# A masked attention and two feed-forward layers on one core: five token blocks in place of six

## The chip, the cores and the metric

The kernel runs on one core of a Trainium2 chip. The metric is the time of one execution in microseconds of the device; the time before is the median of three runs.

## What is computed

```python
scores = scale * np.matmul(q, k.transpose(0, 1, 3, 2))      # q, k, v: 4 x 8 x 576 x 64
kth = np.partition(scores, -32, axis=-1)[..., -32:-31]      # the 32nd largest of each row
scores = np.where(scores >= kth, scores, -1e9)
attn = np.exp(scores - np.max(scores, axis=-1, keepdims=True))
attn = attn / (np.sum(attn, axis=-1, keepdims=True) + 1e-09)
x = np.matmul(attn, v)                                      # -> 2304 tokens x 512
h = np.maximum(x @ w_in, 0.0);  x = (h * h) @ w_out         # layer 0, 512 -> 2048 -> 512
h = x @ w_in2;  out = np.maximum(0.01 * h, h) @ w_out2      # layer 1, other weights
```

## The kernel before, in words

The attention works on 144 tiles of 128 query rows (one head pair's rows of one unit, cut into 128s), two tiles to a **pair**, so 72 pairs, 0 to 71. `UNITS` lists runs of tokens (batch, first token, count) in the order in which they are worked off; a unit of 256 tokens has 8 pairs, one of 320 tokens 10, one of 64 tokens 2. For each pair TensorE multiplies q and k (L279), VectorE finds the 32 largest of each row with four rounds of MAX8 and MATCH_REPLACE8 (L829, L831), ScalarE and GpSimd (POOL in the profile) mask, exponentiate and scale (L298, L299, L303, L312), TensorE transposes (L317, L330) and, when a head pair of a unit is complete, multiplies with V (L412, L401). The result goes to `x_out` (L433 to L436), which splits each value into a high and a low part, xh and xl. For batches 2 and 3 the scores are made early and kept in DRAM.

The two layers run on **blocks** of tokens (`BLOCKS`). A block is ready once its last token has come out of the attention; tokens of a unit that belong to the next block are kept in `spill` and copied by `unspill` (L118, L452, both on POOL). Each layer of a block takes 16 steps f over the 2048 hidden features. A step has 12 matmuls h (L580: four chunks of the 512 inputs, three products of high and low parts) as wide as the block has tokens, then ScalarE and POOL (VectorE in the last block, by `LEAK2` and `GLD`) apply the nonlinearity and split it into gh and gl. In layer 0 it has 12 matmuls acc of the block's width (L618); in layer 1, where gh and gl are the stationary operand, 3 of 512 columns for each 128 tokens (L620). The matmuls acc of a step come one step late (`LAG`).

Block 0 meets the weights for the first time: for its 32 steps they are loaded raw, put together from two 32-bit halves (ScalarE L513, L514, VectorE L518, L519), split (ScalarE L523, POOL L526) and stored to DRAM. Later blocks load 1 MB of split weights for each step.

What sets the order: events have slots, 16 to a pair. At each slot the attention's events are written out, and then as much of the ready block as its `rate` allows, which is its number of matmul groups divided by the number of slots until the next block is ready. When a block becomes ready, what is left of the one before is written out first. The attention's events are put some places forward, and a scheduler then sets the order of each engine, which works its list in that order. `PIPE` says how many blocks run both layers one after the other; the ones behind it are interleaved: in the kernel before, layer 0 of block 4 runs alone, then come layer 0 of block 5, layer 1 of block 4 and layer 1 of block 5. `SETS` says which tiles hold a block's xh and xl: set 0 serves blocks 0, 2 and 4, set 1 blocks 1 and 3, and block 5 has tiles of its own (set 2).

Of the kernel before, what the change touches and what calls it, by code (L numbers as in the profile page):

```python
# [24 lines left out]


UNITS = [
    (0, 0, 256), (0, 256, 256), (0, 512, 64), (1, 0, 256), (1, 256, 320),
    (2, 0, 256), (3, 0, 256), (2, 256, 320), (3, 256, 320),
]  # L30

BLOCKS = [512, 256, 384, 512, 256, 384]

SETS = (0, 1, 0, 1, 0, 2)

PIPE = 4

SPILL = 128


NATIVE = 3
# [22 lines left out]
KLO_D = ((0, 0), (0, 1))  # L64
QLO_D = (0,)

LEAK2 = 5
GLD = 5


@with_exitstack
def topk_attention_moe_moe2_kernel(
# [98 lines left out]
    for i in range(NE):  # L171
        ebufs.append(const.tile([P, S], F, tag=f"e{i}", name=f"e{i}"))
    spill = const.tile([P, NHP, SPILL], F, tag="spill", name="spill")
    early_ctx = ExitStack()
# [195 lines left out]
    g = 0  # L370
    for n in BLOCKS:
        blocks.append(dict(g0=g, n=n, idx=len(blocks)))
# [4 lines left out]
    def block_x(blk):  # L377

        if "x" not in blk:
            i = SETS[blk["idx"]]  # L380
            m = max(x["n"] for x in blocks if SETS[x["idx"]] == i)
            if i == 2:
# [73 lines left out]
    for j in range(len(blocks)):  # L456
        if j < PIPE:
            groups.append([(j, 0), (j, 1)])
        elif j == PIPE:
            groups.append([(j, 0)])  # L460
        else:
            groups.append([(j, 0), (j - 1, 1)])
    if PIPE < len(blocks):
        groups[-1].append((len(blocks) - 1, 1))
# [93 lines left out]
    def moe(j, layer):  # L558
# [6 lines left out]
        for f in range(NF + LAG):  # L565
            conv = iter(())
            if f < NF:
# [21 lines left out]
                if layer == 0:  # L589
                    ACT.activation(a[:, 0:n], h[:, 0:n], AF.Relu)  # L590
                    ACT.activation(a[:, 0:n], a[:, 0:n], AF.Square)
                elif j >= LEAK2:
                    ACT.activation(a[:, 0:n], h[:, 0:n], AF.Copy, scale=0.01)
                    DVE.tensor_tensor(a[:, 0:n], a[:, 0:n], h[:, 0:n], op=OP.max)
                else:
# [4 lines left out]
                ACT.activation(gh[:, 0:n], a[:, 0:n], AF.Copy)  # L600
                (DVE if j >= GLD else POOL).tensor_tensor(gl[:, 0:n], a[:, 0:n], gh.bitcast(F)[:, 0:n],  # L601
                                                          op=OP.subtract)
# [302 lines left out]
```

## Time and profile before

| what | us |
|---|---|
| median of three runs | 1217.16 (1215.74 to 1218.06) |
| the profiled execution | 1214.43 |
| its span, first to last instruction | 1212.6 |
| TensorE busy / VectorE busy | 1135.6 / 946.5 |
| ScalarE busy / POOL busy | 908.9 / 728.1 |

The span is read by stages: attention alone until block 0 is ready, block 0 with the conversion of the weights, blocks beside the attention, and blocks alone after the last pair. Busy time of TensorE is that of pipelined matmuls, so that durations of neighbours overlap; what a matmul costs in a stream is the distance from one start to the next.

### The profile page before, as it was taken

Reading aid. Unit: us, or ns where it says so; the run is one execution under the profiler, and the core shown is the slowest. Engines: PE = TensorE matmul, PEld = TensorE weight load, DVE = VectorE, ACT = ScalarE, POOL = GpSimd, SP = SyncE. Lnnn points to the kernel's source line nnn. Section 1 sums busy time; section 2 is a strip of 40 time slices with the busy share of each in tenths; the row PEclk is TensorE's granted clock in tenths of the full one; section 3 lists DMA queues with packets and bytes.
Section 4 is the critical chain, followed back from the end, with each engine's and each line's share of the span. In section 5 each row is a group of like instructions: output and inputs, shape, how many; then the busy total and the mean of one; then the engine's idle time right before and its main releaser. Section 6 shows DMA issues by size and latency. Waiting matters only on the chain.

```text
span 1212.6 us, 20357 instructions
## 1 busy us (share of the span) xinstructions
PE 1135.6 (94%) x6388; PEld 992.6 (82%) x6388; DVE 946.5 (78%) x1944; ACT 908.9 (75%) x2019; POOL 728.1 (60%) x868
## 2 busy tenths in 40 slices
PE   4788878999789989999999998999999999999998
PEld 3666765887578879989999996888788899998997
DVE  7999999778888899999999999999999920110122
ACT  6889899989999988887877777777777764334322
POOL 7998977667689985477656684545576642004300
PEclk9999997999989999999999999999999999999999
DMA  9665566878889988889988787667576589879974
GB/s 305 232 224 196 197 197 255 279 273 303 307 281 301 315 281 270 291 283 397 343 297 293 279 274 258 213 221 236 182 233 230 192 270 368 259 247 343 350 253 137
DMA packets 110522, 323.24 MB, mean 267 GB/s; under 512 B 17488, under 2 KB 25680, under 8 KB 110416
## 3 DMA queue, kind: packets, MB, share of 16 engines
q1 hardware_dynamic: 107776, 317.24, 77.1%
q10 hardware_dynamic: 2640, 4.72, 1.1%
q8 instruction: 51, 0.84, 0.3%
q14 instruction: 55, 0.45, 0.1%
HBM read 254.54 MB, written 67.37 MB: 265 GB/s over the span
## 4 chain that ended last, share of the span: by engine, by line
PE 54%; ACT 17%; DVE 12%; DMA 4%; POOL 3%; issue 3%; ACTq 0%; SPq 0%; POOLq 0%; DVEq 0%
PE h L580 22%; PE acc L618 11%; PE acc L620 11%; DVE m L829 5%; DVE w L831 4%; PE att L412 3%; PE att L317 3%; ACT e L303 2%; ACT att L514 2%; ACT e L298 1%; ACT wc L513 1%; PE att L401 1%; ACT s L280 1%; ACT stage L280 1%; DVE PTs L323 1%
## 5 line engine op out<-in xcount | busy, mean ns | idle before, releaser
L580 PE MATMUL h<-xh,wi 128*128 128x512 f32 (+2 forms) x1280 | 349.8, 345 | 10.5 <-ACT gb L598 4.4
L829 DVE MAX8 m<-w 128x8 f32<-128x576 f32 x432 | 313.2, 747 | 1.6
L580 PEld LDWEIGHTS h<-xh,wi 128*128 128x128 f32 x1280 | 227.5, 191 | 39.3 <-ACT gb L598 6.2
L601 POOL TENSOR_TENSOR gl<-ga,gh 128x512 fp32r<-128x512 f32 (+2 forms) x160 | 163.0, 1018 | 118.8 <-ACT gh L600 54.0
L299 POOL TENSOR_TENSOR e<-s,e 128x576 f32<-128x576 f32 x144 | 203.2, 1432 | 26.7 <-ACT e L298 24.2
L831 DVE MATCH_REPLACE8 w<-m,w 128x576 f32<-128x576 f32 x288 | 213.1, 742 | 0.8
L580 PE MATMUL h<-xl,wi 128*128 128x512 f32 (+2 forms) x640 | 206.8, 341 | 2.8 <-DVE xl L632 2.6
L618 PE MATMUL acc<-gh,wo 128*128 128x512 f32 (+2 forms) x768 | 154.8, 341 | 0.4 <-ACT gh L600 0.4
L620 PE MATMUL acc<-wo,gh 128*128 128x512 f32 x576 | 151.1, 397 | 0.7 <-ACT gh L600 0.6
L599 POOL TENSOR_TENSOR ga<-ga,gb 128x512 f32<-128x512 f32 (+2 forms) x80 | 81.3, 1017 | 117.0 <-ACT gb L598 116.6
L618 PEld LDWEIGHTS acc<-gh,wo 128*128 128x128 f32 x768 | 125.0, 189 | 10.6 <-ACT gh L600 1.1
L580 PEld LDWEIGHTS h<-xl,wi 128*128 128x128 f32 x640 | 121.0, 190 | 15.3 <-DVE xl L632 5.1
L600 ACT ACTIVATE gh<-ga 128x512 fp32r<-128x512 f32 (+2 forms) x192 | 100.3, 522 | 35.6 <-POOL ga L599 24.2
L303 ACT ACTIVATE e<-e,kf 128x576 f32<-128x576 f32 x144 | 112.4, 781 | 15.6 <-POOL e L299 14.2
L620 PEld LDWEIGHTS acc<-wo,gh 128*128 128x128 f32 x576 | 104.2, 189 | 19.6 <-ACT gh L600 1.2
L298 ACT ACTIVATE e<-s,kf 128x576 f32<-128x576 f32 x144 | 105.8, 777 | 15.4 <-POOL kf L291 13.5
L829 DVE MAX8 m<-s 128x8 f32<-128x576 f32 x144 | 104.5, 747 | 11.9 <-ACT s L280 10.8
L590 ACT ACTIVATE ga<-h 128x512 f32<-128x512 f32 (+2 forms) x96 | 46.8, 487 | 82.5 <-PE h L580 81.8
L831 DVE MATCH_REPLACE8 w<-m,s 128x576 f32<-128x576 f32 x144 | 106.8, 742 | 0.3
L317 PE MATMUL att<-ident,e 128*128 128x128 f32 x576 | 90.3, 285 | 13.1 <-ACT e L303 9.2
L317 PEld LDWEIGHTS att<-ident,e 128*128 128x128 f32 x576 | 70.6, 145 | 27.4 <-ACT e L303 14.9
L312 ACT ACTIVATE e<-e,rc 128x576 f32<-128x576 f32 x108 | 78.0, 770 | 13.6 <-DVE rc L308 13.5
(93 smaller groups left out, 2150.8 us busy)
## 6 DMA issues: line engine op xcount, KB each, us to landing
wi<-wd SPq DMA_DIRECT2D x160, 512.0 KB, 5.0
wo<-wd SPq DMA_DIRECT2D x160, 512.0 KB, 5.2
wraw<-in_w_dram SPq DMA_DIRECT2D x64, 512.0 KB, 5.7
sd<-stage SPq DMA_DIRECT2D x72, 288.0 KB, 2.8
s<-sd SPq DMA_DIRECT2D x72, 288.0 KB, 5.0
wd<-wi SPq DMA_DIRECT2D x32, 512.0 KB, 5.3
wd<-wo SPq DMA_DIRECT2D x32, 512.0 KB, 5.5
kraw<-in_k_dram SPq DMA_DIRECT2D x16, 576.0 KB, 4.6
```

Source lines behind the costliest of these rows:

```text
L298: ACT.activation(e, x, AF.Relu, bias=pr["kf"][:, i:i + 1], scale=-FAR)
L299: cur["pool"] = POOL.tensor_tensor(e, x, e, op=OP.subtract)
L303: ACT.activation(e, e, AF.Exp, bias=pr["nb"][:, i:i + 1], scale=0.125, accum_out=pr["sum"][:, i:i + 1])
L317: PE.transpose(ps[:, j * P:(j + 1) * P], t["e"][:, j * P:(j + 1) * P], ident)
L580: PE.matmul(h[:, 0:n], lhsT=wi[:, w, c * P:(c + 1) * P], rhs=x[c][y][:, 0:n], start=cnt == 0, stop=cnt == 3 * NK - 1)
L599: POOL.tensor_tensor(a[:, 0:n], a[:, 0:n], b[:, 0:n], op=OP.subtract)
L600: ACT.activation(gh[:, 0:n], a[:, 0:n], AF.Copy)
L601: (DVE if j >= GLD else POOL).tensor_tensor(gl[:, 0:n], a[:, 0:n], gh.bitcast(F)[:, 0:n], op=OP.subtract)
L618: PE.matmul(acc[c][:, 0:n], lhsT=wo[:, w, cs], rhs=g[:, 0:n], start=first, stop=last)
L620: PE.matmul(acc[c], lhsT=g[:, cs], rhs=wo[:, w, :], start=first, stop=last)
L829: cur["dve"] = DVE.max(out=m8[:, x, 8 * r:8 * r + 8], in_=t["s"] if r == 0 else t["w"])
L831: cur["dve"] = DVE.match_replace(out=t["w"], in_to_replace=m8[:, x, 8 * r:8 * r + 8], in_values=t["s"] if r == 0 else t["w"], imm_value=NEG)
```

## The change

The six blocks of 512, 256, 384, 512, 256 and 384 tokens become five of 512, 384, 512, 512 and 384. Batch 1 is divided into units of 320 and 256 tokens instead of 256 and 320, so that unit 3 ends with token 896, where block 1 now ends. `PIPE` is 5, so that every block runs its two layers one after the other and none is interleaved. Set 2 is gone: block 4 uses the tiles of blocks 0 and 2. At most 64 tokens spill. `LEAK2` and `GLD` go from 5 to 4, so that they mean the last block as before.

```diff
 UNITS = [
-    (0, 0, 256), (0, 256, 256), (0, 512, 64), (1, 0, 256), (1, 256, 320),
+    (0, 0, 256), (0, 256, 256), (0, 512, 64), (1, 0, 320), (1, 320, 256),
     (2, 0, 256), (3, 0, 256), (2, 256, 320), (3, 256, 320),
 ]
-BLOCKS = [512, 256, 384, 512, 256, 384]
-SETS = (0, 1, 0, 1, 0, 2)
-PIPE = 4
-SPILL = 128
+BLOCKS = [512, 384, 512, 512, 384]
+SETS = (0, 1, 0, 1, 0)
+PIPE = 5
+SPILL = 64
-LEAK2 = 5
-GLD = 5
+LEAK2 = 4
+GLD = 4
```

The blocks are ready after pairs 15, 25, 35, 51, 61 and 71 before, and after pairs 15, 27, 43, 61 and 71 now.

The first place is TensorE from the matmuls with V of pair 42's tiles to the transposes of pair 44 (e_112 and e_113 are pair 43's tiles, e_110 and e_111 pair 44's). Before:

```order
L317 MATMUL att<-ident,e_112 128x128 x4
L618 MATMUL acc<-gl,wo 128x384
L317 MATMUL att<-ident,e_113 128x128 x4
L618 MATMUL acc<-gl,wo 128x384 x3
...
L412 MATMUL att<-PTs,VT 128x256 x8
L618 MATMUL acc<-gh,wo 128x384 x8
L412 MATMUL att<-PTs,VT 128x256
L618 MATMUL acc<-gl,wo 128x384 x4
L317 MATMUL att<-ident,e_110 128x128 x4
L317 MATMUL att<-ident,e_111 128x128 x4
```

and now:

```order
L620 MATMUL acc<-wo,gl 128x512 x3
L580 MATMUL h<-xh_5790,wi 128x512
L412 MATMUL att<-PTs,VT 128x256
L317 MATMUL att<-ident,e_112 128x128 x4
L317 MATMUL att<-ident,e_113 128x128 x4
L330 MATMUL att<-ident,e_112 64x128
L330 MATMUL att<-ident,e_113 64x128
L412 MATMUL att<-PTs,VT 128x256 x9
L317 MATMUL att<-ident,e_110 128x128 x4
L317 MATMUL att<-ident,e_111 128x128 x4
...
L580 MATMUL h<-xh_5790,wi 128x512 x5
```

Before, block 2 (384 columns) runs between the transposes of the two pairs. Now block 1's last matmuls (L620) and three h of block 2 stand ahead of pair 43, no matmul of a block stands between the pairs, and block 2 (xh_5790) goes on behind pair 44.

The second place is VectorE in pair 29 (m_5683 before, m_5429 now; L518 and L519 convert weights, wc). Before:

```order
L829 MAX m_5683<-s_108 128x8
L323 TENSOR_TENSOR PTs<-att,PTs 128x4x128
L829 MAX m_5494<-w 128x8
L831 MATCH_REPLACE w<-m_5683,s_108 128x576
L829 MAX m_5683<-w 128x8
L831 MATCH_REPLACE w<-m_5683,w 128x576
```

and now:

```order
L829 MAX m_5429<-s_108 128x8
L831 MATCH_REPLACE w<-m_5429,s_108 128x576
L829 MAX m_5429<-w 128x8
L323 TENSOR_TENSOR PTs<-att,PTs 128x4x128
L831 MATCH_REPLACE w<-m_5429,w 128x576
L518 SCALAR_TENSOR_TENSOR wc<-att,wc 128x512
L829 MAX m_5429<-w 128x8
L519 SCALAR_TENSOR_TENSOR wc<-att,wc 128x512
```

The conversion, whose last instruction stood just ahead of pair 28's first MAX8, now goes on through pair 29.

The third place is TensorE where the last block's layer 0 ends, behind all of the attention. Before:

```order
L618 MATMUL acc<-gh,wo 128x384 x8
L618 MATMUL acc<-gl,wo 128x384 x4
L580 MATMUL h<-xh_10045,wi 128x256 x8
L580 MATMUL h<-xl_10046,wi 128x256 x4
L618 MATMUL acc<-gh,wo 128x384 x8
L618 MATMUL acc<-gl,wo 128x384 x4
```

and now:

```order
L618 MATMUL acc<-gh,wo 128x384 x8
L618 MATMUL acc<-gl,wo 128x384 x4
L618 MATMUL acc<-gh,wo 128x384 x8
L618 MATMUL acc<-gl,wo 128x384 x4
L580 MATMUL h<-xh_10238,wi 128x384 x8
L580 MATMUL h<-xl_10239,wi 128x384 x4
```

The first h of layer 1 belonged to another block (256 columns) and stood ahead of the last acc; now it belongs to the same block and stands behind it.

## Rows read from the trace of the kernel before

**Rows 1.** The page, busy us (share of the span) of each engine.

```profile
PE 1135.6 (94%) x6388; PEld 992.6 (82%) x6388; DVE 946.5 (78%) x1944; ACT 908.9 (75%) x2019; POOL 728.1 (60%) x868
```

**Rows 2.** Windows by stage: from:to, length, busy us of each engine, clock, DMA.

```profile
0.00:208.80 208.80, 163.62 (x865) 129.47 (x866) 197.67 (x421) 179.45 (x471) 176.84 (x249) 0.94 0.69 229
208.80:448.80 240.00, 226.91 (x1110) 185.26 (x1109) 196.45 (x369) 224.22 (x463) 190.93 (x187) 0.99 0.85 292
448.80:631.40 182.60, 178.91 (x1262) 171.79 (x1261) 180.55 (x382) 149.79 (x352) 110.94 (x145) 1.00 0.89 314
631.40:754.40 123.00, 117.01 (x668) 107.14 (x667) 121.84 (x258) 95.65 (x200) 82.96 (x99) 0.98 0.84 283
754.40:984.00 229.60, 226.61 (x1130) 187.76 (x1129) 217.11 (x457) 177.10 (x347) 131.12 (x142) 1.00 0.66 212
984.00:1207.00 223.00, 222.54 (x1365) 211.18 (x1363) 32.87 (x61) 81.59 (x187) 35.35 (x48) 1.00 0.82 286
```

**Rows 3.** Windows of VectorE's MAX8 alone (L829): from:to, length, busy (count).

```profile
196.10:435.40 239.30, 59.62 (x81) 0.98 0.83 284
435.40:631.40 196.00, 91.81 (x128) 1.00 0.90 315
631.40:728.90 97.50, 45.59 (x64) 0.98 0.84 284
728.90:971.10 242.20, 114.65 (x160) 0.99 0.67 220
```

**Rows 4.** Chain of work that ended last: start, us; twelve matmuls of 512, 384, 256.

```profile
766.23 2.79 PE acc L618 x12
...
972.72 1.45 PE h L580 x12
...
1028.68 2.10 PE h L580 x12
```

**Rows 5.** Timeline of TensorE, hand-over from block 2 to 3: start, us, instructions, idle before.

```profile
739.78 1.11 PE L412 MATMUL att<-PTs,VT 128*128 128x256 f32 x8
740.73 0.86 PE L620 MATMUL acc<-wo,gl 128*128 128x512 f32 x3
...
742.25 1.15 PE L317 MATMUL att<-ident,e 128*128 128x128 f32 x8
743.15 1.66 PE L620 MATMUL acc<-wo,gh 128*128 128x512 f32 x6
...
754.46 1.78 PE L580 MATMUL h<-xh,wi 128*128 128x512 f32 x5
```

**Rows 6.** Timeline and chain at the start of block 0's layer 1.

```profile
336.18 0.79 PE L580 MATMUL h<-xh,wi 128*128 128x512 f32 x1 [3.58 <-ACT gb L598]
...
336.18 5.49 PE h L580 x12
```

**Rows 7.** Timeline of TensorE between block 3's two layers.

```profile
868.41 1.10 PE L580 MATMUL h<-xl,wi 128*128 128x512 f32 x2 [1.15 <-DVE xl L632]
...
870.69 0.51 PE L580 MATMUL h<-xh,wi 128*128 128x512 f32 x1 [0.38 <-ACT gb L598]
```

**Rows 8.** Conversion: VectorE's longest wait; ScalarE's attention lines, busy, mean ns.

```profile
DVE wc L518 <- ACT att L514: 23.8, 18, 3.8
...
L280 ACT ACTIVATE s<-att 128x288 f32<-128x288 f32 x45 | 18.2, 411 | 0.7 <-PE att L279 0.5
L298 ACT ACTIVATE e<-s,kf 128x576 f32<-128x576 f32 x22 | 17.1, 777 | 0.7 <-PE att L330 0.7
L303 ACT ACTIVATE e<-e,kf 128x576 f32<-128x576 f32 x22 | 17.1, 777 | 0.7 <-POOL e L299 0.7
L312 ACT ACTIVATE e<-e,rc 128x576 f32<-128x576 f32 x20 | 14.4, 773 | 0.7 <-DVE rc L308 0.7
```

**Rows 9.** Timeline of POOL where block 2's spilled tokens are copied.

```profile
439.34 0.65 POOL L118 TENSOR_SCALAR xh<-spill 128x64 fp32r<-128x64 f32 x3
```

**Rows 10.** Waits of TensorE after 984: who waited for whom, us, times, longest.

```profile
PE h L580 <- DMA wi<-wd: 0.4, 1, 0.4
```

## The prediction

> **What bounds the kernel now.** I read the page's busy shares first, then a table of windows by stage, then the steps of one line on VectorE, then the timeline of TensorE at one hand-over. A pair is two tiles of 128 query rows; there are 72, numbered 0 to 71, and VectorE runs 8 MAX8 for each.
>
> TensorE is busy for 94% of the span and VectorE for 78% [rows 1], but the stages have different limits [rows 2]. Until 208.8 there is attention alone. From 208.8 to 448.8 block 0 runs with weights that are still being converted: ScalarE is busy 224.2 of 240.0 us, TensorE 226.9, VectorE 196.5, so ScalarE and TensorE are nearly full and VectorE, which could go faster, waits. From 448.8 to 754.4 VectorE is busy 180.6 of 182.6 and 121.8 of 123.0: it sets the pace, and TensorE idles 3.7 and 6.0 us. From 754.4 on TensorE has no more than 3.5 us of idle time until 1207: whatever work it has left then is what the end waits for.
>
> The count of MAX8 gives the pace of the pairs [rows 3]. In the conversion, pairs 18 to 27 take 239.3 us, 23.9 each (80 MAX8; the 81st of that row lies across its edge); the next 16 take 196.0, 12.2 each; 8 more take 97.5, and the last 20 take 242.2, 12.1 each. So pair 44 begins at 631.4 and pair 52 at 728.9.
>
> At 754.46, 25.6 us after pair 52 began, TensorE goes on with block 3, which became complete with pair 51 [rows 5]. From there to its last matmul at 1206.9 are 452.4 us. These two numbers, the 25.6 and the 452.4, carry the sum.
>
> **Prices.** Twelve matmuls take 2.79 us at 512 columns, 2.10 at 384 and 1.45 at 256 [rows 4]: 0.2325, 0.175 and 0.121 us each. A block runs 16 x 36 matmuls of its own width and 16 x 3 of 512 columns for each 128 of its tokens. That is 178.6 us for 512 tokens, 134.3 for 384, 92.0 for 256. A pair of attention costs TensorE 0.90 us for 8 transposes (742.25 to 743.15), about 0.25 for the two short ones and 1.06 for the matmuls with V (8 take 0.95 us, 739.78 to 740.73; nine to a pair) [rows 5]: 2.2 us.
>
> **The change part by part.**
>
> *One block less.* Before, the six blocks cost 2 x (178.6 + 134.3 + 92.0) = 809.8 us of TensorE; after, 3 x 178.6 + 2 x 134.3 = 804.4: 5.4 us less. The tokens are the same, and what goes is the fixed part of a matmul, since 256 columns cost more than half of 512. The Trainium skill (TensorE: Matmul & The Clock Gate, Back-to-back issue gap) gives columns / 2.4 GHz plus 2.5 ns for each matmul; by it 512 columns would cost 215.8 ns, this part would save 1.5 us instead of 5.4, the 86.6 us below would be 82.1 and the predicted time 1216.2. The trace has 232 ns for 512 columns [rows 4] and does not agree, so the sum goes by the trace.
>
> *Loads.* The 32 steps of the block that goes take 64 loads of weights with them. I cost that at nothing: transfers run beside the matmuls, and in the last 223 us TensorE waits for one only once, 0.4 us [rows 10]. That also bounds what their absence can return on the path.
>
> *The point at which blocks become complete.* This is where the change acts. Blocks were complete after pairs 15, 25, 35, 51, 61 and 71; now after 15, 27, 43, 61 and 71. By pair 43 only blocks 0 and 1 (178.6 + 134.3 = 312.9 us) have been on offer, where before three (404.9) had been since pair 35. The order of TensorE shows the result: between the transposes of pairs 43 and 44 no matmul of a block is left. TensorE must wait for attention there and then has block 2, 3 and 4 ahead: 178.6 + 178.6 + 134.3 = 491.5 us. Before, from 754.46, it had blocks 3, 4 and 5: 404.9. That is 86.6 more. It also has 27 pairs of attention ahead instead of 19: 8 x 2.2 = 17.6. So from the hand-over to the end it needs 452.4 + 86.6 + 17.6 = 556.6 us.
>
> If VectorE is no faster than before, the hand-over comes 25.6 us after 631.4, at 657.0, and the last matmul at 1213.6: 6.7 us later than now. The saved 5.4 us and the idle time gained before 657.0 are both inside this number.
>
> *The conversion stretch.* The rate at which block 0 is laid out is set by the pairs until the next block, 12 instead of 10, so about two more pairs share the conversion: the order of VectorE has its last conversion in pair 29 instead of at the start of pair 28. Each of these two no longer costs 12.2 us afterwards. What it costs in the stretch is not in the trace. If TensorE sets it, 3.3 us (2.2 and the scores); if ScalarE does, its work for a pair: two each of 0.78, 0.78 and 0.77 us and four of 0.41 [rows 8] are 6.3, with some 2 us of smaller ones 8.3, at 93% occupancy 8.9; if VectorE's in-order queue does, the whole 12.2. VectorE's longest wait in the stretch is for ScalarE (23.8 us) [rows 8], so I take 8.9 and with it 2 x 3.3, rounded down to 6 us, since the three engines are then loaded more evenly and disturb each other more. The bounds are 0 and 17.
>
> *The end.* Before, block 5's first layer was followed by block 4's second, which waits for nothing. Now block 4's second layer follows its own first, with no attention left to fill the gap. The nearest row is the boundary between block 3's layers: 1.15 and 0.38 us of idle time [rows 7]. I take 1.5; bounds 0 and 1.5.
>
> *A colder start.* After the idle 3.58 us before 336.18, twelve matmuls took 5.49 us instead of 2.79 [rows 6]: TensorE ran at the lower of its two levels, 1.2 GHz. The wait at pairs 43 and 44 is longer than the one at 745 to 754, of which part of such a loss is in the 452.4 already. I add 1.3; bounds 0 and 2.7.
>
> *The x tiles.* Block 4 now reuses the tiles of block 2 (set 0) where block 5 had its own. POOL's copy of the 64 spilled tokens into them stands behind pair 62's subtraction and must wait for block 2's last h matmul; behind it on POOL are block 2's gl, the kf of pair 63 and its subtraction, for which ScalarE's exponentials wait. When block 2's spill went in at 439.34 there was no idle time before it [rows 9]. I take 0; upper bound 5 us, the rest of block 2's last step after pair 61.
>
> *The sum:* 6.7 - 6 + 1.5 + 1.3 = 3.5 us more. The profiled execution lasts 1214.43 us (span 1212.6) and the median of the three runs is 1217.16, so the difference goes on the median: 1220.7.
>
> **The rivals.**
>
> *The conversion gives back more (faster).* If TensorE sets the stretch, two pairs save up to 17 us. From 9.5 us on the kernel is no slower; at 15 the time is 1217.2 + 6.7 - 15 + 2.8 = 1211.7. For it: VectorE idles 43.5 us there. Against: ScalarE is at 93%. Chance 0.17.
>
> *TensorE's sum alone counts (faster).* TensorE is at 94%, so 5.4 us less work would end 5.4 us earlier, at 1211.8. Against: the order empties TensorE at pair 44, and VectorE, at 99%, cannot bring pair 44 sooner by itself. Chance 0.08.
>
> *Nothing comes back, and POOL waits (slower).* The conversion gives 0 and the copy into set 0 stalls POOL: 6.7 + 2.8 + 3 = 12.5, so 1229.7. Chance 0.20.
>
> *The forecast,* gains of 3 to 9 us in the conversion: 1217.7 to 1223.7. Chance 0.55.
>
> **How the numbers follow.** About 0.2%, 2.4 us, is what a measurement of this kernel can tell from no change. Of the forecast's 0.55, some 0.24 lies inside it and the rest is slower; of the first two rivals 0.22 is faster, 0.03 inside or slower; the third is slower. That makes faster 0.22, same 0.25, slower 0.53. The low end, 1210, takes in both faster rivals; the high end, 1231, the third with the bounds of the boundary and of the clock.
>
> **What would show it.** MAX8 of pair 44 near 625 on VectorE (631 if the conversion gave nothing, below 620 for the first rival); some 10 us of idle TensorE just before block 2's first layer; no idle time on TensorE worth naming from there on; 556 us or a little more from there to the last matmul; a tail after the last matmul with V of about 224 us of block work (now 220). It would be wrong if block 2 began before 645, if TensorE idled again after pair 45, or if POOL sat for more than 3 us before its copy from spill.

## The result, and the profile after

The changed kernel takes 1232.89 us (median; 1230.37 to 1233.45) against 1217.61 beside it: 1.0114 of the time before, 95% interval 1.0093 to 1.0136, 14 to 15 us slower. The prediction was 1220.7 us in a range up to 1231. The direction was right; the time lies above the range. The profiled execution took 1230.37 us, its span is 1228.6 and its last matmul ends at 1222.8 (before: 1206.9), so 15.9 us are to be explained in the profiles, of which the prediction had 3.5.

The page, as [rows 1]:

```profile
PE 1142.4 (93%) x5812; PEld 968.0 (79%) x5812; DVE 948.3 (77%) x1940; ACT 897.7 (73%) x1915; POOL 717.8 (58%) x812
```

TensorE has 576 matmuls and 5.4 us of work less than before, and yet is busy 6.8 us longer: its matmuls ran slower (mean granted clock of the span 0.974, before 0.983). The windows by stage of the kernel after; columns as in [rows 2], the stages cut at its own points: block 0 until 474.0, block 1 until pair 44, the hand-over, blocks beside attention, blocks alone.

```profile
0.00:208.80 208.80, 164.31 (x865) 129.78 (x866) 197.80 (x421) 179.26 (x470) 177.28 (x249) 0.94 0.69 228
208.80:474.00 265.20, 245.95 (x1197) 201.12 (x1197) 227.78 (x435) 247.82 (x512) 201.71 (x195) 0.97 0.79 274
474.00:631.40 157.40, 155.59 (x925) 146.72 (x924) 151.38 (x316) 121.24 (x262) 96.83 (x115) 1.00 0.77 261
631.40:658.80 27.40, 18.48 (x92) 14.88 (x90) 27.02 (x58) 19.17 (x38) 15.07 (x21) 0.75 0.63 213
658.80:984.00 325.20, 320.95 (x1572) 265.94 (x1572) 308.17 (x648) 245.98 (x476) 182.20 (x197) 0.98 0.66 222
984.00:1222.80 238.80, 237.14 (x1170) 209.52 (x1168) 36.13 (x66) 83.11 (x159) 44.67 (x37) 1.00 0.61 207
```

The fourth row is the new wait: in 27.40 us TensorE is busy 18.48, at a granted clock of 0.75, while VectorE is busy 27.02. It is where the prediction put it. Its timeline on TensorE (start, us, instructions, in brackets the idle time before and who ended it):

```profile
643.12 0.39 PE L412 MATMUL att<-PTs,VT 128*128 128x256 f32 x1 [1.13 <-DVE PTs L340]
647.88 1.97 PE L317 MATMUL att<-ident,e 128*128 128x128 f32 x8 [4.38 <-ACT e L312]
...
652.51 2.58 PE L412 MATMUL att<-PTs,VT 128*128 128x256 f32 x9 [2.23 <-DVE PTs L323]
655.80 1.97 PE L317 MATMUL att<-ident,e 128*128 128x128 f32 x8 [0.71 <-ACT e L312]
658.22 0.64 PE L330 MATMUL att<-ident,e 128*64 128x128 f32 x2 [0.45 <-DVE xf L418]
658.76 2.50 PE L580 MATMUL h<-xh,wi 128*128 128x512 f32 x5
```

Block 2 goes on at 658.76, not 651, and its first five matmuls take 2.50 us where those of block 3 took 1.78 [rows 5]. The eight transposes take 1.97 us for both pairs. In the kernel before, those of pair 51 took 1.15 [rows 5], but those of pair 52, just ahead of the block, took 1.97 too:

```profile
752.41 1.97 PE L317 MATMUL att<-ident,e 128*128 128x128 f32 x8 [1.28 <-ACT e L312]
754.17 0.63 PE L330 MATMUL att<-ident,e 128*64 128x128 f32 x2
```

The windows of VectorE's MAX8 (L829), as [rows 3], for pairs 30 to 37 before, then for pairs 30 to 37 and 38 to 43 now (66 MAX8 where two neighbours lie across the edges):

```profile
461.20:560.20 99.00, 45.93 (x66) 1.00 0.87 301
...
452.80:559.70 106.90, 46.19 (x64) 1.00 0.73 247
559.70:631.20 71.50, 33.79 (x48) 1.00 0.83 287
```

Pair 30 begins at 452.8, where before it was 461.2: 8.4 us gained in the conversion. But the next 8 pairs take 106.9 us, 13.4 each instead of 12.4, and pair 44 begins at 631.2, as before. From 475 to 550 TensorE is busy for every microsecond of three windows of 25, and what VectorE waits for most between 450 and 562 is ScalarE's copy of scores (L280):

```profile
DVE m L829 <- ACT s L280: 4.0, 4, 1.4
```

Behind the hand-over TensorE loses time where layers change. Between block 2's two layers it waits for VectorE's xl, and the matmuls behind it come 0.43 us apart instead of 0.23, at a granted clock of 0.50, the lower level; between block 4's two layers it waits for ga, and the clock stays at 1.00 (the windows of both places stand last):

```profile
772.98 0.50 PE L580 MATMUL h<-xl,wi 128*128 128x512 f32 x1 [0.83 <-DVE xl L632]
774.17 0.49 PE L580 MATMUL h<-xl,wi 128*128 128x512 f32 x1 [0.69 <-DVE xl L632]
...
776.43 0.63 PE L580 MATMUL h<-xl,wi 128*128 128x512 f32 x1
776.86 0.63 PE L580 MATMUL h<-xh,wi 128*128 128x512 f32 x1
...
1157.43 0.44 PE L580 MATMUL h<-xh,wi 128*128 128x384 f32 x1 [1.17 <-DVE ga L594]
...
776.00:781.00 5.00, 5.00 (x12) 3.86 (x13) 5.00 (x14) 2.25 (x4) 2.51 (x2) 0.50 0.26 97
1153.30:1157.40 4.10, 2.96 (x12) 2.05 (x12) 2.47 (x5) 1.57 (x4) 0.00 (x0) 1.00 0.56 190
```

For all kernels below I use one ledger. The **lost time** of a stretch is its length less its matmuls of TensorE at their warm price (the distance from one start to the next that each shape has in the trace of before); it holds idle time and the lower clock alike. By stage, us:

| stage | before | after | units alone | all serial | other blocks |
|---|---|---|---|---|---|
| 208.8 to 450 | 24.8 | 31.3 | 35.9 | 24.1 | 25.3 |
| 450 to 740 | 10.4 | 25.8 | 14.9 | 12.5 | 12.0 |
| 740 to 985 | 15.0 | 9.4 | 4.2 | 15.9 | 16.3 |
| 985 to the last matmul | 1.7 | 5.6 | 1.4 | 5.9 | 7.3 |
| last matmul ends | 1206.9 | 1222.8 | 1211.8 | 1214.1 | 1216.8 |

(Until 208.8 all lose 84 to 85.) The change saves some 4 us of work by this ledger and loses 20 us more.

### The profile page after: what moved, and what is told of

Same layout as the page of the kernel before. It is cut to its first block, busy times and chain, and to the rows that moved or that the text cites. A ratio compares the mean times of both kernels' runs of the same rounds, so it can differ in the third digit from the quotient of the medians.

```text
span 1228.6 us, 18794 instructions
## 1 busy us (share of the span) xinstructions
PE 1142.4 (93%) x5812; PEld 968.0 (79%) x5812; DVE 948.3 (77%) x1940; ACT 897.7 (73%) x1915; POOL 717.8 (58%) x812
## 4 chain that ended last, share of the span: by engine, by line
PE 51%; DVE 21%; ACT 13%; POOL 3%; issue 3%; DMA 2%; ACTq 0%; SPq 0%; POOLq 0%
PE h L580 22%; PE acc L620 12%; DVE m L829 9%; PE acc L618 8%; DVE w L831 7%; PE att L317 2%; PE att L412 2%; DVE PTs L323 2%; ACT e L303 2%; PE att L401 2%; DMA wraw<-in_w_dram 1%; ACT wc L513 1%; ACT stage L280 1%; POOL e L299 1%; ACT att L514 1%
## 5 line engine op out<-in xcount | busy, mean ns | idle before, releaser
L580 PE MATMUL h<-xh,wi 128*128 128x512 f32 (+1 forms) x1280 | 406.9, 381 | 17.8 <-ACT ga L590 6.1
L829 DVE MAX8 m<-w 128x8 f32<-128x576 f32 x432 | 313.8, 748 | 2.0
L580 PEld LDWEIGHTS h<-xh,wi 128*128 128x128 f32 x1280 | 238.7, 190 | 59.6 <-ACT ga L590 8.7
L580 PE MATMUL h<-xl,wi 128*128 128x512 f32 (+1 forms) x640 | 237.4, 377 | 2.3 <-DVE xl L632 2.2
L601 POOL TENSOR_TENSOR gl<-ga,gh 128x512 fp32r<-128x512 f32 (+1 forms) x128 | 157.0, 1227 | 120.7 <-ACT gh L600 70.0
L618 PE MATMUL acc<-gh,wo 128*128 128x512 f32 (+1 forms) x640 | 154.4, 380 | 3.9 <-ACT gh L600 3.9
L620 PE MATMUL acc<-wo,gh 128*128 128x512 f32 x576 | 149.2, 398 | 0.5 <-ACT gh L600 0.5
L601 DVE TENSOR_TENSOR gl<-ga,gh 128x384 fp32r<-128x384 f32 x32 | 17.9, 558 | 151.5 <-ACT gh L600 151.5
L618 PEld LDWEIGHTS acc<-gh,wo 128*128 128x128 f32 x640 | 117.5, 191 | 20.0 <-ACT gh L600 4.8
L303 ACT ACTIVATE e<-e,kf 128x576 f32<-128x576 f32 x144 | 112.3, 781 | 17.8 <-POOL e L299 17.2
L600 ACT ACTIVATE gh<-ga 128x512 fp32r<-128x512 f32 (+1 forms) x160 | 94.1, 588 | 41.5 <-POOL ga L599 29.9
L620 PEld LDWEIGHTS acc<-wo,gh 128*128 128x128 f32 x576 | 105.7, 188 | 21.8 <-ACT gh L600 1.0
L599 POOL TENSOR_TENSOR ga<-ga,gb 128x512 f32<-128x512 f32 (+1 forms) x64 | 78.5, 1227 | 69.2 <-ACT gb L598 61.3
L829 DVE MAX8 m<-s 128x8 f32<-128x576 f32 x144 | 104.2, 748 | 11.0 <-ACT s L280 9.8
L590 ACT ACTIVATE ga<-h 128x512 f32<-128x512 f32 (+1 forms) x80 | 44.3, 553 | 69.7 <-PE h L580 69.3
```

The source lines that it names most:

```text
L303: ACT.activation(e, e, AF.Exp, bias=pr["nb"][:, i:i + 1], scale=0.125, accum_out=pr["sum"][:, i:i + 1])
L580: PE.matmul(h[:, 0:n], lhsT=wi[:, w, c * P:(c + 1) * P], rhs=x[c][y][:, 0:n], start=cnt == 0, stop=cnt == 3 * NK - 1)
L599: POOL.tensor_tensor(a[:, 0:n], a[:, 0:n], b[:, 0:n], op=OP.subtract)
L618: PE.matmul(acc[c][:, 0:n], lhsT=wo[:, w, cs], rhs=g[:, 0:n], start=first, stop=last)
L620: PE.matmul(acc[c], lhsT=g[:, cs], rhs=wo[:, w, :], start=first, stop=last)
L829: cur["dve"] = DVE.max(out=m8[:, x, 8 * r:8 * r + 8], in_=t["s"] if r == 0 else t["w"])
```

## Experiments

**Theories.** A: the hand-over at pairs 43 and 44 makes the loss, since block 2 is complete only then and all the rest comes after it. B: spreading the conversion over 12 pairs makes it. C: the serial tail makes it. D: TensorE's work as a whole sets the end, wherever it lies.

**The parts alone.** The division of batch 1 alone, in the kernel before:

```diff
-    (0, 0, 256), (0, 256, 256), (0, 512, 64), (1, 0, 256), (1, 256, 320),
+    (0, 0, 256), (0, 256, 256), (0, 512, 64), (1, 0, 320), (1, 320, 256),
```

> The kernel before with the new division of batch 1 alone (320 tokens first, then 256): block 1 is ready two pairs later, so block 0 and its conversion are spread over 12 pairs as in the kernel after, but there are still six blocks and block 2 is complete early enough that TensorE has work at pair 44. Theory A (the loss comes from the hand-over at pairs 43 and 44, where TensorE runs out of block work): within -5 to +3 us of the kernel before. Rival B (the loss comes from spreading the conversion over 12 pairs and from what follows it up to pair 38): 8 us or more slower than before. By both, VectorE starts pair 30 some 8 us earlier than before, as in the kernel after.

It measured 1222.94 us, 1.0037 (1.0020 to 1.0055): 4.5 us slower, between the two. Theory A's limit of +3 is passed. The ledger (third column) shows why: the conversion loses 11 us more of TensorE than before, but as TensorE is late it no longer runs dry ahead of block 3, and 10.8 us come back between 740 and 985. Pair 30 begins at 457.6, 3.6 us earlier than before (8 expected). Pairs 30 to 37 then take 99.5 us, and pair 44 begins at 627.4, 4 us earlier than before (631.5; in the run with all blocks serial 634.2): with a block 1 of 256 tokens the gain of the spreading reaches pair 44.

All six blocks one after the other, in the kernel before (`PIPE` 4 to 6):

> The kernel before with PIPE = 6: all six blocks run their two layers one after the other, so the last blocks have the boundary between layers of the kernel after, and nothing else changes until the last pair. Theory A: the boundaries cost 1 to 2 us each, +1.5 to +3 us over before. Rival C (the serial tail is what made the kernel after slower): +10 us or more.

1220.89 us, 1.0032 (1.0011 to 1.0054): 3.9 us, and 4.2 more lost behind 985. C is out as the main cause; the boundaries cost more than the 1.5 to 3 expected.

The last two blocks interleaved again, in the kernel after (`PIPE` 5 to 3):

> The kernel after with PIPE = 3, so that the last two blocks interleave their layers again (block 4's layer 0 between block 3's two). Theory A: the boundary inside block 4 (2.2 us of idle time in the trace of after) is hidden, so 1 to 3 us faster than the kernel after, still 12 us or more slower than before. Rival C: most of the 15 us come back, near the kernel before.

1232.62 us, 1.0118 (1.0081 to 1.0155): no gain. Both miss (and the idle time at that boundary is 1.2 us in the trace, not 2.2); the interleaved blocks lose 3.4 us between 985 and 1040 where the serial ones lose 2.0.

Other blocks in the kernel before, so that its own dry place ahead of block 3 goes:

```diff
-BLOCKS = [512, 256, 384, 512, 256, 384]
+BLOCKS = [512, 256, 384, 256, 512, 384]
-SETS = (0, 1, 0, 1, 0, 2)
+SETS = (0, 1, 0, 1, 2, 0)
```

> The kernel before with the blocks 512, 256, 384, 256, 512, 384 instead of 512, 256, 384, 512, 256, 384: the fourth block is ready after pair 43 instead of 51, so TensorE has work through pairs 44 to 52, where the kernel before idles 6.0 us. Six blocks and the old division of batch 1 stay. Theory A (a block that is ready too late costs the idle time at the hand-over, the cold start behind it and nothing else): 3 to 6 us faster than before. Rival B (the end is set by what TensorE and VectorE do elsewhere, the hand-over is covered): same as before within 2 us.

1222.39 us, 1.0034 (1.0015 to 1.0053): slower, a miss for A as it was put. The old dry place is gone (0.6 us lost between 740 and 780 instead of 9.1), but the smaller fourth block is used up before the next is complete, and TensorE waits there:

```profile
875.57 3.84 PE L580 MATMUL h<-x,wi 128*128 128x512 f32 x9 [3.82 <-ACT x L433]
```

A block that is ready earlier is only a gain if the one behind it is ready when it is done.

The old division of batch 1 in the kernel after (with `SPILL` 256), so that block 1 is ready after pair 35:

> The kernel after with the old division of batch 1 (256 tokens first, then 320): block 1 is then complete only after pair 35 instead of 27, block 2 as before after pair 43, so the hand-over without block work moves to pair 35, with 623 us of blocks and some 88 us of attention ahead of TensorE. Theory A: pair 35 begins at about 505 on VectorE, its hand-over comes 27 us later, so the last matmul is near 1244 and the time 1245 to 1265, at least 12 us slower than the kernel after. Rival B (spreading the conversion is what costs, or pays, and block readiness counts little): within 8 us of the kernel after.

1273.03 us, 1.0444 (1.0414 to 1.0474): 40 us slower than the kernel after. The sign is A's, the size beyond its range: from block 1's start at 543.38 to the last matmul at 1265 are 722 us (712 expected), but that start came 48 us after pair 35 began on VectorE, not 27.

```profile
543.38 1.97 PE L580 MATMUL h<-xh,wi 128*128 128x384 f32 x5 [3.24 <-ACT xh L433]
```

**Work left out on either side of the hand-over,** in the kernel after. Each is this edit with another condition:

```diff
+                if (j, layer) == (1, 1) and f >= 4:
+                    mm = [m for m in mm if m[2] == 0]
```

Ahead of it, in block 1's layer 1:

> The kernel after, with work left out ahead of the hand-over: in 12 of the 16 steps of block 1's layer 1 the four h matmuls with xl are left out, 48 of 384 columns, 8.4 us of TensorE. Theory A (the end is set by when block 2 is complete and by what TensorE has ahead from there): TensorE runs dry 8 us earlier at pairs 42 to 44 and the end stays within 1.5 us of the kernel after. Rival D (TensorE's whole work sets the end, and its idle time at pair 44 only moves): 6 to 8 us faster than the kernel after.

1233.38 us, 1.0111 (1.0077 to 1.0145): nothing gained, as A has it. The counterpart, with (3, 1) and 4 <= f < 13:

> The counterpart of the run before it: the kernel after, with the same amount left out behind the hand-over, in 9 steps of block 3's layer 1 the four h matmuls with xl, 36 of 512 columns, 8.4 us of TensorE. Theories A and D alike: 7 to 9 us faster than the kernel after. If TensorE waited for attention there (a rival E, that VectorE with its 72 pairs sets the end of block 3), less than 4 us.

1223.91 us, 1.0042 (1.0029 to 1.0056): 8 to 9 us faster. What lies behind the hand-over counts in full.

VectorE's work left out ahead of it:

```diff
+            if r == 2 and 41 <= p <= 43:
+                pass
```

> The kernel after with VectorE's work left out ahead of the hand-over: in pairs 41, 42 and 43 the third of the four rounds of MAX8 and MATCH_REPLACE8 is left out (the mask then keeps 24 instead of 32 in these rows), 3 x 2 x 1.33 = 8 us of VectorE. Theory A (the hand-over follows VectorE's pairs): pair 44 begins 6 to 8 us earlier, block 2 begins 4 to 8 us earlier, the time is 4 to 8 us shorter than that of the kernel after. Rival D (TensorE's whole work sets the end): within 1.5 us of the kernel after.

1226.45 us, 1.0076 (1.0064 to 1.0088): 5 to 6 us faster. Pair 44 begins at 622.6, 8.6 us earlier than in the kernel after, and block 2 goes on at 653.19 instead of 658.76, 5.6 earlier. TensorE's matmuls are the same, so by D nothing should have moved; by A the attention brings the hand-over, and the end moves with it.

18 matmuls more, put into the first wait (4.4 us):

> The kernel after with 18 matmuls of 512 columns more at the end of block 1's layer 1, whose sum is not used: 4.2 us of TensorE placed into the 4.4 us that it waits ahead of pair 43's transposes. Theory A with a cost of the cold clock (of the 14.6 us lost between 631 and 660, 8.9 are idle and the rest is the lower clock): the transposes and the first matmuls of block 2 run warm, 1 to 4 us faster than the kernel after. Rival (the lower clock behind the hand-over comes whatever fills one of the waits, or the filling only delays pair 43's transposes): same as after within 1 us, or up to 4 us slower.

1231.52 us, 1.0105 (1.0077 to 1.0134): within 1.5 us of the kernel after, where D would have them cost 4.2. The granted clock of 631.4 to 660 rises from 0.74 to 0.87 (the window of after, then of this run), but block 2 still goes on at 659.26, and its first five matmuls still take 2.50 us: the waits behind the filled one remain. The lower clock in the filled wait is not what delays the hand-over.

```profile
631.40:660.00 28.60, 19.68 (x94) 15.89 (x93) 28.19 (x60) 19.55 (x39) 15.78 (x21) 0.74 0.65 219
```

```profile
631.40:660.00 28.60, 22.95 (x113) 18.32 (x112) 28.20 (x61) 20.16 (x40) 16.19 (x22) 0.87 0.65 222
```

**The conversion.** Block 0's rate worked out for 32 slots fewer, in the kernel after:

```diff
-        rate.append(sum(quanta(*ph) for ph in groups[j]) / max(nxt - rslot[j] - 1, 40))
+        rate.append(sum(quanta(*ph) for ph in groups[j]) / max(nxt - rslot[j] - 1 - (32 if j == 0 else 0), 40))
```

> The kernel after, with the rate of block 0 worked out for two pairs fewer, so that block 0 and the conversion are done by pair 27 as in the kernel before: the spreading over 12 pairs is undone and nothing else. Theory A (what the spreading gives VectorE by pair 30 is lost again by pair 38): pair 30 begins near 461 as before, pair 44 near 631, the time within 1.5 us of the kernel after. Rival B (the spreading costs): 4 us or more faster than the kernel after. The prediction's own term (the spreading gives 6 us): 4 to 8 us slower.

1230.44 us, 1.0114 (1.0099 to 1.0128): the ratio of the kernel after, as A has it. Pair 30 begins at 459.9 instead of 452.8, the next 8 pairs take 98.9 us instead of 106.9, and pair 44 begins at 631.7 instead of 631.2:

```profile
459.90:558.80 98.90, 45.76 (x64) 0.97 0.69 220
```

What the spreading gives VectorE by pair 30 is gone by pair 38. Is TensorE's work there the reason? Block 1's layer 0 with less of it, (1, 0) and f >= 1:

> The kernel after with work left out where the conversion's gain was lost again: in 15 of 16 steps of block 1's layer 0 (pairs 28 to 36) the four h matmuls with xl are left out, 60 of 384 columns, 10.5 us of TensorE. Theory A with the reading that TensorE paces pairs 30 to 38 (25 of 25 us busy between 475 and 500 and between 525 and 550): pairs 30 to 38 come closer together, pair 44 begins 4 to 8 us earlier than in the kernel after, and since the hand-over goes with pair 44 the time is 3 to 8 us shorter. Rival (VectorE or ScalarE sets those pairs, the gain was never one for pair 44): pair 44 within 1.5 us of after, and as in the run that left work out in layer 1 no gain, within 1.5 us of the kernel after.

1221.92 us, 1.0044 (1.0031 to 1.0057), 8.5 us faster by the ratios, yet not for the reason given: pair 44 begins at 632.0, and pairs 30 to 37 take 104.8 us, only 2.1 less. The cut did not empty TensorE there: from 475 to 525 it is still busy for every microsecond, so the question stays open. In its profile block 2 goes on earlier because its matmuls stand ahead of pair 44's transposes on TensorE:

```profile
654.70 2.50 PE L582 MATMUL h<-xh,wi 128*128 128x512 f32 x5 [2.79 <-ACT xh L433]
```

So the last four runs asked whether it is the order. The kernel after once more:

> The kernel after once more, unchanged, beside the next three on one chip: what one execution differs from another. All theories: 1.0114 of before within 0.0025; the hand-over 27 to 28 us after pair 44 begins on VectorE, and some 597 us from pair 44's begin to the end of the span, whenever pair 44 begins.

1232.67 us, 1.0130 (1.0109 to 1.0151), as expected. Four steps of layer 1 cut, (1, 1) and f >= 12, with the order as it was:

> The kernel after with the h matmuls with xl left out in the last 4 steps of block 1's layer 1, 16 of 384 columns, 2.8 us of TensorE ahead of the hand-over. On TensorE pair 44's transposes still stand ahead of block 2's sixth and later matmuls, as in the kernel after. Reading F (work cut ahead of the hand-over is idle time there; a gain in such runs came from the order of TensorE's queue): hand-over 27 to 28 us after pair 44 begins, within 1.5 us of the kernel after. Rival D (TensorE's work counts wherever it is): 2 to 3 us faster.

1229.02 us, 1.0093 (1.0073 to 1.0114): 3.7 us faster than the run before it, D's size rather than F's. The lag that F had at 27 to 28 us is 25.5. Five steps, f >= 11:

> The same with one step more left out, 5 steps, 3.5 us; this step tips the order: block 2's matmuls now stand ahead of pair 44's transposes, and at the next hand-over, pair 62 to 63, only 2.1 us of block work stand on TensorE between the pairs' transposes (8.4 in the kernel after). Reading F: block 2 goes on 22 to 24 us after pair 44 begins instead of 27 to 28, and up to 5 of these us are lost again as idle time near pair 63, so between 5 us faster than the kernel after and no change. Rival (the order at pair 44 does not matter, attention's own chain sets it): hand-over still 27 to 28 us after pair 44 begins.

1232.72 us, 1.0121 (1.0103 to 1.0139): no change, though block 2 goes on 23.6 us after pair 44 begins. The gain is lost again where block 3 is waited for, and the run that cut 8.4 us shows the same place (first the five steps, then that run):

```profile
884.22 0.41 PE L330 MATMUL att<-ident,e 128*64 128x128 f32 x2 [3.17 <-DVE xf L418]
```

```profile
887.47 0.63 PE L330 MATMUL att<-ident,e 128*64 128x128 f32 x2 [3.43 <-DVE xf L418]
```

Eight steps of layer 0, (1, 0) and f >= 8, with the order as it was:

> The kernel after with the h matmuls with xl left out in the last 8 steps of block 1's layer 0, 32 of 384 columns, 5.6 us, in pairs 31 to 36; pair 44's transposes stand ahead of block 2's matmuls as in the kernel after. Reading F: within 2 us of the kernel after, since what is cut there is idle time at pair 44 too. Rival G (TensorE's work in pairs 30 to 38 holds VectorE back and counts one for one): 4 to 6 us faster, with pair 44 on VectorE as much earlier.

1224.44 us, 1.0051 (1.0033 to 1.0069): 8.2 us faster for 5.6 us of work. Both readings miss: F by the time, G because pair 44 begins at 631.1, no earlier than in the first profile of the kernel after and 2.2 earlier than in the second. The profiles, us (lag: from pair 44's begin on VectorE to block 2 going on; stretch: from there to the last matmul):

| kernel | pair 44 | lag | stretch | lost in the stretch |
|---|---|---|---|---|
| after | 631.2 | 27.6 | 564.0 | 18.1 |
| after, again | 633.3 | 27.9 | 564.0 | 18.0 |
| 18 matmuls more | 631.7 | 27.6 | 563.8 | 17.8 |
| layer 1, 12 steps cut | 637.5 | 23.6 | 567.5 | 20.3 |
| layer 1, 5 steps cut | 634.4 | 23.6 | 567.2 | 20.1 |
| layer 1, 4 steps cut | 634.2 | 25.5 | 559.7 | 13.8 |
| layer 0, 8 steps cut | 631.1 | 25.6 | 561.1 | 14.9 |
| layer 0, 15 steps cut | 632.0 | 22.7 | 562.7 | 15.4 |

Against the first profile of the kernel after, the point at which block 2 goes on moves by -2.1, -4.1, -0.7, +0.9 and +2.3 us for cuts of 5.6, 10.5, 3.5, 2.8 and 8.4; against the second, which ran beside three of these cuts, by -4.5, -6.5, -3.2, -1.5 and -0.1. So how much of a cut is lost again as waiting at the hand-over, as A says, depends on the profile it is held against. The lag depends on it less: it is shorter by 2 to 5 us in all five. Each cut also deals the queues anew, and the lost time behind changes with them, from 4.3 us less to 2.2 us more. Three of the five cuts gained what D would give or nearly so (3.7 for 2.8, 8.2 for 5.6, 8.5 for 10.5), two gained nothing; the table puts the gains into the lag, the boundary behind and, in part, an execution with an earlier pair 44. These pieces are as large as what the last four runs were to tell apart, and the profiled executions are not the median ones (4 steps of layer 1: 1226.94 us for a median of 1229.02; 12 steps: 1236.16 for 1233.38; 15 steps of layer 0: 1224.89 for 1221.92). Which piece of order is worth what was not isolated and stays open.

## Why the prediction was wrong in size

The sum was for a last matmul at 1210.4; it came at 1222.8, 12.4 us later. By the steps:

- **The late hand-over (6.7): right in kind.** It lies between pairs 43 and 44. With less of VectorE's work before it, it came 5.6 us earlier and the time fell by 5 to 6 us; 18 matmuls more before it cost nothing; what was left out behind it counted in full. That TensorE's work before it costs nothing is not shown: two cuts there gained nothing, three gained 3.7 to 8.5 us. The 86.6 and 17.6 us of work held: the 564.0 us hold 545.9 of work, where the prediction's 452.4 (10.0 of it lost) plus 104.2 make 546.6. The 25.6 us of lag did not: 27.6, and that is 2 us. The transposes of pair 44 begin 24.6 us after the pair, where those of pair 52 began 23.5 after theirs, and block 2 goes on 2.96 us behind them instead of 2.05, with a wait of 0.45 for VectorE's xf. The lower clock alone does not explain it: pair 52's transposes took 1.97 us as well, and with pair 43's in 1.32 us (the run with 18 matmuls more) the lag was the same. Which wait adds the 1.1 us ahead of them stays open.
- **The conversion gives 6 back: wrong, the largest part.** The gain is there at pair 30 (8.4 us) and not at pair 44 (0.3). The run that undoes the spreading gives the same ratio. The step that failed is "each of these two no longer costs 12.2 us afterwards": it took the start of pair 30 for finished work and let the pairs behind it run at 12.2 us. In the trace of pairs 30 to 37 they take 13.4: VectorE's idle time is 5.7 us instead of 1.3, 4.0 of it for scores, and it is busy for 3.5 us more, of which 1.4 are two additions of PTs (L323) still owed from the pairs before. [Rows 2] had 3.7 us of idle time in 182.6 for TensorE there, little room for more; but that a full TensorE holds the scores back is not shown. In the runs with the units alone and with the spreading undone it is busy for every microsecond from 475 to 525 too, and VectorE waits there for less than 1 us in pairs 30 to 37. This is 5.7 us.
- **TensorE in the conversion: missing.** That the spreading costs TensorE time (31.3 lost instead of 24.8, and 35.9 in the run with the units alone) was no term. Here it costs little: the run that undoes the spreading loses 7.7 us less until 450 and 7.2 more from there to 740.
- **The boundary (1.5) and the cold start (1.3): too small.** The lost time behind the hand-over is 18.1 us, against 12.8 by the prediction (10.0 + 2.8). I priced the boundary within block 4 (2.5 measured) but let the one within block 2 go, which now lies behind the hand-over beside attention: 4.8 us, with xl queued on VectorE between MAX8s. [Rows 7] had the pattern, 1.15 and 0.38 us of idle time, and I took the idle time for the price. In the kernel before that boundary loses 3.7 us between 862 and 876, at a clock of 1.00, in part because the record of a matmul lasts 0.39 us where it costs 0.23, so that idle time counted from its end is less than the time lost. Within block 2 the lower clock comes on top. About 5 us.
- **POOL's copy from spill (0, bound 5): right.** The wait is there, 0.5 us:

```profile
POOL xh L118 <- PE h L580: 0.5, 1, 0.5
```

- **The rivals.** Of the two faster ones nothing is seen. "Nothing comes back, and POOL waits" (1229.7) was nearest: nothing came back, but POOL did not wait; lag and boundaries took its place. The range ended at 1231 because it had no bound for the lag and counted the boundary at no more than 1.5.
- **What would show it.** The begin of pair 44 at 631 is the sign that the text names for a conversion that gave nothing. Idle time ahead of block 2 is 8.9 us in 631.4 to 658.8 (some 10 said), and the tail after the last matmul with V is 224 us, as said; the stretch is 564 instead of 556.6; "no idle time from there on" is wrong at 772 and 1157.

5.7 + 2.0 + 5.3 (lost) - 0.7 (work) make 12.3 of the 12.4 us. This is the bookkeeping of two profiles; by experiment only the first term is shown (the run with the spreading undone).

## To carry to other kernels

Where one engine takes work that becomes available in lumps, ask at each lump how long the queue lasts and when the next lump comes; saving work ahead of such a point can buy nothing (8.4 us cut here, none gained), though three other cuts did gain; and a lump that is split elsewhere moves the gap rather than closing it. Follow a gain on the pacing engine into the next stage before you carry it forward: here 8.4 us were gone fourteen pairs later. A boundary costs more than the idle time of its rows: 1.2 and 1.5 us of it stood for 2.5 and 3.7 us at full clock; within block 2, where the clock fell to 0.50 behind it, 4.8 were lost. Price it by the distance from one start to the next.

## What was not expected of the hardware

Executions with the same order of instructions differ by several us before the end of the conversion, and keep the difference. In the first 208.8 us, with attention alone, the granted clock was 0.94 in the profile of the kernel after and 0.91 in that of the same program run again:

```profile
0.00:208.80 208.80, 167.50 (x859) 132.74 (x860) 196.58 (x417) 178.50 (x468) 177.27 (x249) 0.91 0.69 227
```

Pair 30 began at 452.8 and 454.8, pair 44 at 631.2 and 633.3, and the span ended at 1228.6 and 1230.9: from pair 44 on both take 597 us. With the last blocks interleaved (0.92 in that stage) it was 456.3, 634.6 and 1231.2. The six executions of the program run again, on one chip, took 1229.87 to 1236.66 us. So one profile against one other can show some 3 us that belong to the execution and not to the change.
